# Attention and a two-layer MLP on one core: keys in four even tiles from the tenth pair on, in a newly drawn plan

## The chip, the core and the metric

One NeuronCore of a Trainium2 chip runs the whole program. Its engines work side by side, each through its own list of instructions in order: TensorE (PE) multiplies matrices, VectorE (DVE), ScalarE (ACT) and GpSimd (POOL) work on elements, and SyncE (SP) issues transfers, as ACT and POOL can too. Engines wait for each other by semaphores. The metric is the device time of one execution in microseconds (us). The kernel before took 692.31 us, the median of 3 runs (692.15 to 693.16).

## What is computed

```python
def _attn_ref(q, k, v, cap):                      # q, k, v: 4 x 12 heads x 448 x 64
    scale = 1.0 / np.sqrt(q.shape[-1])
    scores = scale * np.matmul(q, k.transpose(0, 1, 3, 2))
    scores = cap * np.tanh(scores / cap)          # cap = 30
    scores = scores - np.max(scores, axis=-1, keepdims=True)
    attn = np.exp(scores)
    attn = attn / (np.sum(attn, axis=-1, keepdims=True) + 1e-09)
    return np.matmul(attn, v)

def _moe_ref(x, w_in, w_out):                     # x: 1792 x 768, w_in: 768 x 2048, w_out: 2048 x 768
    h = x @ w_in
    g = np.maximum(0.01 * h, h)
    return g @ w_out
```

The heads of a batch, laid side by side, are the rows of x.

## The kernel before

**Pairs.** Two heads make a pair; there are 24, six for each of the four batches. Head 0 of a pair stands on partitions 0 to 63 of a tile, head 1 on 64 to 127. Keys and queries are loaded in 32-column pieces and turned on DVE (kT, qT, 128 x 448). The scores are computed with keys on the partitions, so that tanh (`L414`) and exp (`L416`) on ACT write the probabilities `pf` just as the product with the values needs them. 448 keys are three tiles of 128 and a rest of 64. For the three, one matmul for each head reads half of the partitions (`L406`, two side by side); the two rests share one tile: `kb` is a block matrix with both rests on its diagonal, and one full 128 x 128 matmul (`L403`) makes their scores. Values come in eight blocks (`vc`, four DMAs); for each of the four tiles two matmuls of 64 columns add to `po0` (`L434`). The sums of exp are added up on DVE or POOL in `t` (`L450` to `L454`) and multiplied with ones on PE (`L459`, `po1`). DVE turns the sums, takes the reciprocal, turns it back and scales (`L467` to `L479`).

**The MLP.** It runs in single-pass matmuls (`m`, `L543`) on numbers split into a rounded part and the rest: x into xh and xl, g into gh and gl, weights into two parts in `w` (`split`, the helpers `L234`, `L238` and `L241`: a cast on ACT or DVE, then a subtraction on DVE or POOL). Three products for each 128 rows. A unit is one block of 128 columns of the first layer (six blocks of rows, 18 matmuls) or one block of the second for a chunk of 5 or 6; 34 units a batch, 136 in all. In the first batch a weight is loaded raw (`wr`), its bits rearranged by ACT and DVE (`L528` to `L535`), and stored to `scratch`, from where later batches load it (`ws`). ACT or DVE makes 0.01 h (`L578`), DVE the maximum (`L583`); second-layer blocks are accumulated in `late` (`L592`), turned (`L600`) and stored by SP in four DMAs (`L605`).

**The order** is no scheduler's on the chip: class `Plan` lays it out while the program is built. Each step is added with a rank (a due time by pair or unit, shifted by the tables `role`, `pair` and `unit`), the engines that could do it, a cost for each, what it reads and writes, and a `mode` (the tiling of PE that its matmuls need). `issue` repeats: of the steps whose inputs are there, take the one that can start first (in steps of 0.1 us, then by rank), on the engine where it would end first, with the penalties in `phases` added for some engines; a step of PE in another mode than the last costs `SWITCH` more. What comes out is one fixed list for each engine. Rings of buffers (`raw` 3, `kT` 2, `w` 4, `pf` 4, `g` 11 and so on) say how far a step may run ahead of its reader.

Of the kernel before, what the change touches and what calls it, by code (L numbers as in the profile page):

```python
# [14 lines left out]
ALU = mybir.AluOpType  # L15
# [9 lines left out]
    pf=4,  # L25
# [29 lines left out]
    phases=[(-496.0, 3.97, 0.03), (5863.0, 0.58, 1.0), (1000000000.0, 7.89, 3.45)],  # L55
# [7 lines left out]
class Plan:  # L63
# [9 lines left out]
    SWITCH = 10  # L73
# [93 lines left out]
def softcap_attention_mlp(  # L167
# [87 lines left out]
    ring("vx", 2, [P, 4, 3, D])  # L255
# [83 lines left out]

    way = lambda i: "whole" if i < T["np"] else "beside"  # L340
# [37 lines left out]
    def plan_pair(i):  # L378
        plan.part("pair", " zero" if i == 0 else " first" if i < NP else "", i)
        r0 = 10.0 * i  # L380
        how = way(i)
# [10 lines left out]
        for j in range(2):  # L392
            plan.add(r0 + T["pk"] + 1, {"dve": 0.15, "act": 0.25, "pool": 0.5}, lambda e, j=j: copy(
                e, at("kb", i)[half[j], half[j]], at("kT", i)[half[j], mid_keys[j]], zeros[half[j]]), [("kT", i)], [("kb", i)])
        plan.add(r0 - T["al"] + 1, {"sp": 1.05 if how == "whole" else 2.1}, lambda e: load_v(i), [("fixed_vx", 0)], [("vx" if how == "whole" else "vc", i)], xfer=1.05)

        last = []
        for g in range(NG):
            ver = NG * i + g

            def scores(e, g=g, ver=ver):
                if g == MID:
                    nc.tensor.matmul(at("sc", ver)[:, 0, 0:S], at("kb", i), at("qT", i), start=True, stop=True)  # L403
                    return
                for j in range(2):
                    nc.tensor.matmul(at("sc", ver)[:, j, 0:S], at("kT", i)[half[j], tile_keys(j, g)], at("qT", i)[half[j]], start=True, stop=True)  # L406

            plan.add(r0 + T["pq"] + 2 * g, {"pe": BOTH}, scores, ([("kb", i)] if g == MID else [("kT", i)]) + [("qT", i)], [("sc", ver)], mode=int(g != MID))
            n = 1 if g == MID else 2
            sc = lambda ver=ver, n=n: at("sc", ver)[:, 0:n, 0:S]  # L410
            pf = lambda ver=ver, n=n: at("pf", ver)[:, 0:n]
            r = r0 + T["pt"] + 2 * g
            ct = 0.15 + 0.37 * n
            a = plan.add(r, {"act": ct}, lambda e, sc=sc, pf=pf: nc.scalar.activation(pf(), sc(), AF.Tanh, scale=inv_sb),  # L414
                         [("sc", ver), ("inv", 0)], [("pf", ver)])
            plan.add(r, {"act": ct + 0.03}, lambda e, pf=pf: nc.scalar.activation(pf(), pf(), AF.Exp, scale=cap_sb), (), [("pf", ver)], after=[a])  # L416


            r = r0 + T["pp"] + 2 * g
            if how == "whole":  # L420
                def values(e, g=g, ver=ver):
                    for j in range(2):
                        c = slice(0, P) if g < MID else half[j]
                        t = at("vx", i)[c, (g if j == 0 else g + 1) if g < MID else (3, 0)[j], j:j + 2]
                        nc.tensor.matmul(at(f"po{j}", i)[:, 0:S], t.rearrange("p o d -> p (o d)"), at("pf", ver)[c, j if g < MID else 0],
                                         start=(g == 0), stop=(g == MID))

                last = [plan.add(r, {"pe": 2 * BOTH if g < MID else BOTH + 0.1}, values, [("vx", i), ("pf", ver)], [("po0", i), ("po1", i)],
                                 after=last, mode=int(g == MID))]
            else:  # L430
                def values(e, g=g, ver=ver):
                    for j in range(2):
                        c = 3 + j if g == MID else g + 5 * j
                        nc.tensor.matmul(at("po0", i)[half[j], 0:S], at("vc", i)[:, c], at("pf", ver)[:, j if g < MID else 0],  # L434
                                         start=(g == 0), stop=(g == MID))
# [312 lines left out]
```

## Time and profile before

| | us |
|---|---|
| median of 3 runs | 692.31 |
| the profiled execution, its own time | 692.5 |
| its span (first to last instruction in the trace) | 690.7 |
| PE busy, share of the span | 668.9, 97% |
| DVE busy | 459.5, 67% |
| ACT busy | 416.2, 60% |
| POOL busy | 90.3, 13% |

Matmuls are pipelined, and the ends in the trace are modelled: how much PE really does is read from start to start. An fp32 matmul of the attention shows as two records, those of the MLP as one.

### The profile page before, as it was taken

Reading aid. Unit: us, or ns where it says so; the run is one execution under the profiler, and the core shown is the slowest. Engines: PE = TensorE matmul, PEld = TensorE weight load, DVE = VectorE, ACT = ScalarE, POOL = GpSimd, SP = SyncE. Lnnn points to the kernel's source line nnn. Section 1 sums busy time; section 2 is a strip of 40 time slices with the busy share of each in tenths; the row PEclk is TensorE's granted clock in tenths of the full one; section 3 lists DMA queues with packets and bytes.
Section 4 is the critical chain, followed back from the end, with each engine's and each line's share of the span. In section 5 each row is a group of like instructions: output and inputs, shape, how many; then the busy total and the mean of one; then the engine's idle time right before and its main releaser. Section 6 shows DMA issues by size and latency. Waiting matters only on the chain.

```text
span 690.7 us, 9078 instructions
## 1 busy us (share of the span) xinstructions
PE 668.9 (97%) x3136; PEld 496.3 (72%) x3136; DVE 459.5 (67%) x667; ACT 416.2 (60%) x612; POOL 90.3 (13%) x115
## 2 busy tenths in 40 slices
PE   8898999999999999999999999999999999999994
PEld 4234657766778557557888977788987499999983
DVE  4987999799989768775465547544456657345552
ACT  5997989798787777775452435544326625444330
POOL 8422221014200521220000000000000000000000
PEclk9999999999999999999999999999999999999998
DMA  9988879887885847533223254522333146333324
GB/s 137 195 139 210 224 224 269 274 222 220 227 277 196 191 105 137 121 88 106 92 92 109 80 128 121 150 87 87 103 102 94 37 119 176 95 121 107 100 54 68
DMA packets 173925, 98.20 MB, mean 142 GB/s; under 512 B 130864, under 2 KB 155440, under 8 KB 173872
## 3 DMA queue, kind: packets, MB, share of 16 engines
q1 hardware_dynamic: 169968, 93.65, 52.2%
q0 software_dynamic: 2048, 3.67, 2.8%
q8 instruction: 26, 0.43, 0.3%
q10 hardware_dynamic: 1856, 0.23, 0.3%
q14 instruction: 27, 0.22, 0.1%
HBM read 79.43 MB, written 18.09 MB: 141 GB/s over the span
## 4 chain that ended last, share of the span: by engine, by line
PE 82%; ACT 7%; DVE 5%; DMA 3%; issue 1%; ACTq 0%; DVEq 0%
PE m L543 64%; PE po L434 8%; PE sc L406 6%; PE sc L403 2%; ACT pf L414 2%; PE po L459 2%; ACT pf L416 1%; DVE wr L532 1%; DMA wr<-in_moe_w_in_dram 1%; DVE w L241 1%; DMA vc<-in_v_dram 1%; DVE ws L535 1%; ACT ws L530 1%; ACT wr L528 1%; ACT w L234 1%
## 5 line engine op out<-in xcount | busy, mean ns | idle before, releaser
L543 PE MATMUL m<-xh,w 128*128 128x448 f32 x768 | 231.8, 374 | 1.2 <-DVE late L583 1.1
L543 PE MATMUL m<-gh,w 128*128 128x448 f32 x768 | 229.4, 371 | 0.8 <-DVE w L241 0.6
L241 DVE TENSOR_TENSOR w<-ws,w 128x768 fp32r<-128x768 f32 (+1 forms) x135 | 127.4, 948 | 83.9 <-ACT w L234 76.8
L234 ACT CAST w<-ws 128x768 fp32r<-128x768 f32 (+1 forms) x130 | 102.6, 795 | 130.5 <-PE m L543 115.1
L543 PEld LDWEIGHTS m<-xh,w 128*128 128x128 f32 x768 | 145.0, 189 | 29.5 <-issue 7.1
L543 PEld LDWEIGHTS m<-gh,w 128*128 128x128 f32 x768 | 144.1, 188 | 29.4 <-issue 9.4
L543 PE MATMUL m<-gl,w 128*128 128x448 f32 x384 | 140.4, 366 | 1.2 <-DVE gl L241 1.2
L543 PE MATMUL m<-xl,w 128*128 128x448 f32 x384 | 140.9, 367 | 0.0
L414 ACT ACTIVATE pf<-sc,inv_sb 128x896 f32<-128x896 f32 (+1 forms) x87 | 76.6, 911 | 11.1 <-PE po L434 5.1
L416 ACT ACTIVATE pf<-pf,cap_sb 128x896 f32<-128x896 f32 (+1 forms) x87 | 80.2, 950 | 0.4
L543 PEld LDWEIGHTS m<-gl,w 128*128 128x128 f32 x384 | 72.2, 188 | 7.7 <-DVE gl L241 1.5
L543 PEld LDWEIGHTS m<-xl,w 128*128 128x128 f32 x384 | 72.6, 189 | 7.1 <-issue 1.5
L406 PE MATMUL sc<-qT,kT 64*128 64x448 f32 x288 | 68.0, 573 | 6.5 <-ACT pf L414 4.5
L434 PE MATMUL po<-pf,vc 128*64 128x448 f32 x348 | 74.2, 549 | 0.0
L578 ACT ACTIVATE late<-m 128x448 f32<-128x448 f32 x64 | 34.6, 542 | 42.2 <-PE m L543 38.4
L592 DVE TENSOR_TENSOR late<-m,late 128x448 f32<-128x448 f32 x48 | 29.5, 618 | 43.1 <-PE m L543 42.8
L583 DVE TENSOR_TENSOR late<-m,late 128x448 f32<-128x448 f32 x64 | 39.4, 617 | 26.9 <-ACT late L578 26.7
L406 PEld LDWEIGHTS sc<-qT,kT 64*128 64x128 f32 x288 | 23.3, 185 | 40.1 <-issue 13.4
L434 PEld LDWEIGHTS po<-pf,vc 128*64 128x64 f32 x348 | 22.3, 136 | 41.1 <-issue 35.0
L347 POOL DMA_DIRECT2D qraw<-in_q_dram x64 | 40.3, 636 | 74.6 <-DVE qT L370 48.1
L241 DVE TENSOR_TENSOR gl<-late,gh 128x448 fp32r<-128x448 f32 x61 | 38.5, 636 | 17.0 <-ACT gh L234 16.5
L234 ACT CAST gh<-late 128x448 fp32r<-128x448 f32 x55 | 31.0, 565 | 27.3 <-DVE late L583 26.8
(62 smaller groups left out, 504.6 us busy)
## 6 DMA issues: line engine op xcount, KB each, us to landing
ws<-scratch SPq DMA_DIRECT2D x66, 384.0 KB, 3.1
wr<-in_moe_w_in_dram SPq DMA_DIRECT2D x16, 768.0 KB, 6.5
ws<-scratch SPq DMA_DIRECT2D x36, 320.0 KB, 2.9
scratch<-ws SPq DMA_DIRECT2D x22, 384.0 KB, 5.6
wr<-in_moe_w_out_dram SPq DMA_DIRECT2D x12, 640.0 KB, 5.0
kraw<-in_k_dram SPq DMA_DIRECT2D x96, 56.0 KB, 3.4
vc<-in_v_dram SPq DMA_DIRECT2D x48, 96.0 KB, 3.9
wr<-in_moe_w_out_dram SPq DMA_DIRECT2D x6, 768.0 KB, 7.0
```

Of the source, the lines that this page charges most:

```text
L234: nc.scalar.copy(o, i)
L241: ENG[eng].tensor_tensor(out=o, in0=a, in1=f32(b), op=ALU.subtract)
L347: engine.dma_start(out=t[p0:p0 + 32], in_=src[b, 2 * hp + h, :, 32 * x:32 * x + 32].rearrange("(s i) d -> i s d", i=32),)
L403: nc.tensor.matmul(at("sc", ver)[:, 0, 0:S], at("kb", i), at("qT", i), start=True, stop=True)
L406: nc.tensor.matmul(at("sc", ver)[:, j, 0:S], at("kT", i)[half[j], tile_keys(j, g)], at("qT", i)[half[j]], start=True, stop=True)
L414: a = plan.add(r, {"act": ct}, lambda e, sc=sc, pf=pf: nc.scalar.activation(pf(), sc(), AF.Tanh, scale=inv_sb), [("sc", ver), ("inv", 0)], ...
L416: plan.add(r, {"act": ct + 0.03}, lambda e, pf=pf: nc.scalar.activation(pf(), pf(), AF.Exp, scale=cap_sb), (), [("pf", ver)], after=[a])
L434: nc.tensor.matmul(at("po0", i)[half[j], 0:S], at("vc", i)[:, c], at("pf", ver)[:, j if g < MID else 0], start=(g == 0), stop=(g == MID))
L543: nc.tensor.matmul(o, l, r, start=(first and m == 0), stop=(last and m == len(mm) - 1))
L578: nc.scalar.mul(at("g", f), ps(), 0.01)
L583: plan.add(rank, {"dve": 0.54}, lambda e: nc.vector.tensor_tensor(out=at("g", f), in0=ps(), in1=at("g", f), op=ALU.max), [("m", m)], [("g" ...
L592: op = plan.add(rank, {"dve": 0.54}, lambda e: nc.vector.tensor_tensor(out=acc(), in0=ps(), in1=acc(), op=ALU.add), [("m", m)], [(tag, b)] ...
```

## The change

From pair 9 on (`ev=9`) the 448 keys of a head are four tiles of 112. Scores are eight matmuls on halves in two steps of the plan (four matmuls each), without `kb`; tanh and exp always take two times 448 columns; t takes three wide additions; values (eight matmuls) and sums (two) are one step; v is one DMA. The branch `whole`, which was off (`np=0`), and its buffers `vx` are gone; the ring `pf` has six buffers of its own for four. In the plan a change of mode costs 0.2 us where it cost 0.1; the penalties are given by engine, in four phases, and their limits now fall inside the program; all tables of shifts have other numbers. The last two DMAs of the last output go out by ACT's queue.

```diff
-    pf=4,
+    pf=6,
...
-    np=0,
...
-    phases=[(-496.0, 3.97, 0.03), (5863.0, 0.58, 1.0), (1000000000.0, 7.89, 3.45)],
+    phases=[(40.0, {'pool': 0.43, 'dve': 0.3, 'act': 5.66}), (100.0, {'pool': 0.21, 'dve': 0.5, 'act': 0.05}), (200.0, {'dve': 0.51, 'act': 0.33, 'sp': 5.98}), (1000000000.0, {'dve': 0.5, 'sp': 14.02})],
+    ev=9,
...
-    SWITCH = 10
+    SWITCH = 20
...
+    KT = S // NG
+    even = lambda i: i >= T["ev"]
...
+        if even(i):
+            rows = v[b, 2 * hp:2 * hp + 2].rearrange("h s d -> (h s) d").rearrange("(c p) d -> p c d", p=KT)
+            nc.sync.dma_start(out=at("vc", i)[0:KT], in_=rows)
             return
...
+        K = KT if even(i) else P
+        wide = lambda g: 2 if even(i) or g < MID else 1
+        pf = lambda g: at("pf", NG * i + g)[0:K, 0:wide(g)]
...
+        def scores(g):
+            if wide(g) == 1:
+                nc.tensor.matmul(at("sc", NG * i + g)[:, 0, 0:S], at("kb", i), at("qT", i), start=True, stop=True)
+                return
+            for j in range(2):
+                keys = slice(KT * g, KT * g + KT) if even(i) else tile_keys(j, g)
+                nc.tensor.matmul(at("sc", NG * i + g)[0:K, j, 0:S], at("kT", i)[half[j], keys], at("qT", i)[half[j]], start=True, stop=True)
...
+        for gs in ((0, 1), (2, 3)) if even(i) else ((0,), (1,), (2,), (3,)):
+            keys = [("kT", i)] if wide(gs[0]) == 2 else [("kb", i)]
+            plan.add(r0 + T["pq"] + 2 * gs[0], {"pe": len(gs) * BOTH}, each(scores, gs), keys + [("qT", i)], vers("sc", gs), mode=int(wide(gs[0]) == 2))
...
+        if even(i):
+            def all_values(e):
+                each(values, range(NG))(e)
+                total(e)
+
+            plan.add(r0 + T["pp"] + 7, {"pe": (NG + 1) * BOTH}, all_values, vers("pf", range(NG)) + [("vc", i), ("t", i), ("fixed_vx", 0)], [("po0", i), ("po1", i)], mode=2)
...
                 for r in range(4):
-                    nc.sync.dma_start(
+                    queue = nc.scalar if m == B * NU - 1 and r >= 2 else nc.sync
+                    queue.dma_start(
```

On PE, in the middle of the program, the steps of a pair between two runs of m matmuls (sc are scores, with kT on halves of the array and with kb on the whole of it; po are values, and sums where ones stand). Before:

```order
L543 MATMUL m_159<-gh_138,w_134 128x448
L406 MATMUL sc_88<-qT_81,kT_79 128x448 x2
L406 MATMUL sc_89<-qT_81,kT_79 128x448 x2
L434 MATMUL po_0_90<-pf_94,vc_86 64x448 x2
L434 MATMUL po_0_90<-pf_95,vc_86 64x448 x2
L406 MATMUL sc_88<-qT_81,kT_79 128x448 x2
L403 MATMUL sc_89<-qT_81,kb_83 128x448
L459 MATMUL po_0_91<-t_96,ones 64x448 x2
L543 MATMUL m_159<-gh_139,w_134 128x448
```

And a pair at about the same place now:

```order
L533 MATMUL m_160<-gh_141,w_133 128x448
L406 MATMUL sc_86<-qT_81,kT_79 112x448 x2
L406 MATMUL sc_87<-qT_81,kT_79 112x448 x2
L411 MATMUL po_0_88<-pf_90,vc_84 64x448 x2
L411 MATMUL po_0_88<-pf_91,vc_84 64x448 x2
L411 MATMUL po_0_88<-pf_92,vc_84 64x448 x2
L411 MATMUL po_0_88<-pf_93,vc_84 64x448 x2
L415 MATMUL po_0_89<-t_96,ones 64x448 x2
L406 MATMUL sc_86<-qT_81,kT_79 112x448 x2
L406 MATMUL sc_87<-qT_81,kT_79 112x448 x2
L533 MATMUL m_159<-gh_137,w_134 128x448
```

Six changes of tiling for seven steps before, four for nine now; over the whole program 151 and 141.

On DVE, while the first units of the MLP run between the pairs 7 and 8 (late is g here, gh and gl its two parts, w the weight's). Before:

```order
L583 TENSOR_TENSOR late<-m_159,late 128x448
L535 SCALAR_TENSOR_TENSOR ws_131<-ws_131,wr_128 128x768
L241 TENSOR_TENSOR gl_151<-late,gh_140 128x448
L532 SCALAR_TENSOR_TENSOR wr_127<-wr_127 128x768
L241 TENSOR_TENSOR w_132<-ws_131,w_132 128x768
L583 TENSOR_TENSOR late<-m_160,late 128x448
L535 SCALAR_TENSOR_TENSOR ws_130<-ws_130,wr_127 128x768
```

Now, at the same work:

```order
L573 TENSOR_TENSOR late<-m_160,late 128x448
L469 TENSOR_TENSOR x_103<-po_0_88,sums_99 128x448
L238 CAST gh_142<-late 128x448
L238 CAST w_132<-ws_131 128x768
L241 TENSOR_TENSOR xl_121<-x_103,xh_110 128x448
L241 TENSOR_TENSOR w_132<-ws_131,w_132 128x768
L573 TENSOR_TENSOR late<-m_159,late 128x448
L367 STREAM_TRANSPOSE kT_78<-kraw_73 128x448
L238 CAST gh_141<-late 128x448
```

Casts that stood in ACT's list (gh, w) now stand in DVE's.

In the list of SP, the stores at the end of the program (out_dram is the output; late, kraw and qraw are the buffers that it is stored from). Before:

```order
L605 DMA out_dram<-late 32x14x32 x4
L605 DMA out_dram<-kraw_73 32x14x32 x4
L605 DMA out_dram<-late 32x14x32 x4
L605 DMA out_dram<-qraw_76 32x14x32 x4
L605 DMA out_dram<-kraw_74 32x14x32 x4
L605 DMA out_dram<-qraw_77 32x14x32 x4
```

Now:

```order
L596 DMA out_dram<-late 32x14x32 x4
L596 DMA out_dram<-kraw_73 32x14x32 x4
L596 DMA out_dram<-late 32x14x32 x4
L596 DMA out_dram<-qraw_76 32x14x32 x4
L596 DMA out_dram<-kraw_74 32x14x32 x4
L596 DMA out_dram<-qraw_77 32x14x32 x2
```

The other two of the last output stand behind ACT's last cast.

## Rows read from the trace of the kernel before

**Rows 1.** The page: span, and busy time by engine, its share, instructions.
```profile
span 690.7 us, 9078 instructions
PE 668.9 (97%) x3136; PEld 496.3 (72%) x3136; DVE 459.5 (67%) x667; ACT 416.2 (60%) x612; POOL 90.3 (13%) x115
```

**Rows 2.** Busy time by stretches: stretch, length, each engine (instructions), clock, DMA, GB/s.
```profile
0.00:143.00 143.00, 132.73 (x586) 76.44 (x588) 119.38 (x173) 123.04 (x174) 42.38 (x63) 0.99 0.92 208
143.00:225.00 82.00, 80.84 (x377) 57.07 (x374) 76.67 (x107) 66.36 (x100) 15.12 (x13) 1.00 0.76 231
...
300.00:551.00 251.00, 251.00 (x1199) 199.25 (x1199) 140.09 (x204) 123.66 (x184) 9.15 (x11) 1.00 0.35 99
551.00:691.00 140.00, 129.35 (x637) 118.72 (x633) 68.14 (x99) 48.23 (x75) 1.15 (x1) 0.97 0.40 104
```

**Rows 3.** PE's waits: who waited for whom, us in total, times, longest.
```profile
PE sc L406 <- ACT pf L414: 4.5, 3, 2.9
```

**Rows 4.** Timeline of ACT from 58 us: start, us, instruction, idle before.
```profile
58.18 0.94 ACT L530 ACTIVATE ws<-wr 128x768 f32<-128x768 f32 x1
62.58 0.90 ACT L528 ACTIVATE wr<-wr 128x768 int32<-128x768 uint8 x1 [3.46 <-DMA wr<-in_moe_w_in_dram]
```

**Rows 5.** Timeline of PE from 60 us.
```profile
64.42 1.02 PE L406 MATMUL sc<-qT,kT 64*128 64x448 f32 x4 [2.87 <-ACT pf L414]
65.37 0.47 PE L543 MATMUL m<-xh,w 128*128 128x448 f32 x1
...
69.83 0.54 PE L403 MATMUL sc<-qT,kb 128*128 128x448 f32 x1
```

**Rows 6.** Timeline of PE from 376 us.
```profile
376.58 0.36 PE L543 MATMUL m<-gl,w 128*128 128x448 f32 x1
376.78 0.37 PE L543 MATMUL m<-gh,w 128*128 128x448 f32 x1
377.08 1.77 PE L406 MATMUL sc<-qT,kT 64*128 64x448 f32 x8
378.78 0.47 PE L543 MATMUL m<-xh,w 128*128 128x448 f32 x1
379.09 0.37 PE L543 MATMUL m<-xl,w 128*128 128x448 f32 x1
```

**Rows 7.** Groups by line and shape: busy us, mean ns of one, idle before.
```profile
L416 ACT ACTIVATE pf<-pf,cap_sb 128x896 f32<-128x896 f32 x65 | 66.5, 1045 | 0.3
L414 ACT ACTIVATE pf<-sc,inv_sb 128x896 f32<-128x896 f32 x65 | 63.6, 1006 | 10.1 <-PE po L434 5.1 <-PE sc L406 4.6
...
L234 ACT CAST gh<-late 128x448 fp32r<-128x448 f32 x55 | 31.0, 565 | 27.3 <-DVE late L583 26.8
...
L416 ACT ACTIVATE pf<-pf,cap_sb 128x448 f32<-128x448 f32 x22 | 14.7, 670 | 0.1
L414 ACT ACTIVATE pf<-sc,inv_sb 128x448 f32<-128x448 f32 x22 | 13.9, 631 | 1.0 <-PE sc L403 0.9
...
L238 DVE CAST gh<-late 128x448 fp32r<-128x448 f32 x9 | 3.4, 382 | 0.1
```

**Rows 8.** Timelines of POOL and DVE near 175 us; w on DVE: min/median/max ns.
```profile
175.38 2.13 POOL L450 TENSOR_TENSOR t<-pf,pf 128x896 f32<-128x896 f32 x1 [8.54 <-issue]
...
175.43 2.76 DVE L241 TENSOR_TENSOR w<-ws,w 128x640 fp32r<-128x640 f32 x1
...
L241 DVE TENSOR_TENSOR w<-ws,w x135: 782/950/2760, 51.8 to 672.1; 128x768 fp32r<-128x768 f32 x88, 128x640 fp32r<-128x640 f32 x47
```

**Rows 9.** Timeline of PE, SP and DVE at the end; SPq is SP's issuing.
```profile
680.19 0.36 PE L543 MATMUL m<-gh,w 128*128 128x448 f32 x1
680.43 3.21 SPq L605 DMA_DIRECT2D out_dram<-kraw  x4
...
681.25 0.65 DVE L600 STREAM_TRANSPOSE qraw<-late 128x448 f32<-128x448 f32 x1
683.75 2.02 SPq L605 DMA_DIRECT2D out_dram<-qraw  x4
```

More of the change, by code (lines that the diff above doesn't have):

```diff
@@ L391, in plan_pair @@
                      [(nm + "raw", i)], [(nm + "T", i)], port=False)
[L392 to L397, printed above, removed]
@@ L398, in plan_pair @@
-        for g in range(NG):
[L399 to L411, printed above, removed]
-            r = r0 + T["pt"] + 2 * g
[L413 to L435, printed above, removed]
-                last = [plan.add(r, {"pe": BOTH}, values, [("vc", i), ("pf", ver)], [("po0", i)], after=last, mode=2)]
@@ new lines, in plan_pair @@
+        plan.add(r0 - T["al"] + 1, {"sp": 0.55 if even(i) else 2.1}, lambda e: load_v(i), [("fixed_vx", 0)], [("vc", i)], xfer=1.05)
+        if not even(i):
+            for j in range(2):
+                plan.add(r0 + T["pk"] + 1, {"dve": 0.15, "act": 0.25, "pool": 0.5}, lambda e, j=j: copy(
+                    e, at("kb", i)[half[j], half[j]], at("kT", i)[half[j], mid_keys[j]], zeros[half[j]]), [("kT", i)], [("kb", i)])
+        K = KT if even(i) else P
+        wide = lambda g: 2 if even(i) or g < MID else 1
@@ new lines, in values, with total, each, do @@
+        def values(g):
+            for j in range(2):
+                c = NG * j + g if even(i) else 3 + j if g == MID else g + 5 * j
+                nc.tensor.matmul(at("po0", i)[half[j], 0:S], at("vc", i)[0:K, c], pf(g)[:, j if wide(g) == 2 else 0], start=(g == 0), stop=(g == NG - 1))
+        def total(e):
+            for j in range(2):
+                nc.tensor.matmul(at("po1", i)[half[j], 0:S], ones[0:K], tt()[:, j], start=True, stop=True)
+        def each(fn, gs):
+            def do(e):
+                for g in gs:
+                    fn(g)
+            return do
@@ new lines, in plan_pair @@
+        WIDE = {"dve": 1.0, "pool": 2.25}
+        r = r0 + T["pt"] + 3
+        a = plan.add(r, WIDE, lambda e: ENG[e].tensor_tensor(out=tt(), in0=pf(0), in1=pf(1), op=ALU.add), vers("pf", [0, 1]), [("t", i)])
+        for g in range(2, NG):
+            if wide(g) == 2:
+                a = plan.add(r + 2 * g - 2, WIDE, lambda e, g=g: ENG[e].tensor_tensor(out=tt(), in0=tt(), in1=pf(g), op=ALU.add), vers("pf", [g]), [("t", i)], after=[a])
+                continue
+            for j in range(2):
+                plan.add(r + 4, {"dve": 0.65, "pool": 1.3}, lambda e, j=j, g=g: ENG[e].tensor_tensor(
+                    out=tt()[half[j], j], in0=tt()[half[j], j], in1=pf(g)[half[j], 0], op=ALU.add), vers("pf", [g]), [("t", i)], after=[a])
@@ new lines, in plan_pair @@
+        if even(i):
[3 more added lines that the diff above has]
+            plan.add(r0 + T["pp"] + 7, {"pe": (NG + 1) * BOTH}, all_values, vers("pf", range(NG)) + [("vc", i), ("t", i), ("fixed_vx", 0)], [("po0", i), ("po1", i)], mode=2)
+        else:
+            last = []
+            for g in range(NG):
+                last = [plan.add(r0 + T["pp"] + 2 * g, {"pe": BOTH}, each(values, [g]), vers("pf", [g]) + [("vc", i)], [("po0", i)], after=last, mode=2)]
+            plan.add(r0 + T["pp"] + 7, {"pe": BOTH}, total, [("t", i), ("fixed_vx", 0)], [("po1", i)], mode=2)
@@ L472, in plan_pair @@
             [("rt", i)], [("sums", 2 * i + 1)], port=False)
[L473 to L481 removed]
+        plan.add(rn, {"dve": 0.54}, lambda e: nc.vector.tensor_tensor(
+            out=at("x", 2 * i + 1), in0=at("po0", i)[:, 0:S], in1=at("sums", 2 * i + 1), op=ALU.mult),
+            [("po0", i), ("sums", 2 * i + 1)], [("x", 2 * i + 1)], port=False)
         split(rn + 0.5, lambda: at("xh", i), lambda: at("xl", i), lambda: at("x", 2 * i + 1), S, [("x", 2 * i + 1)], ("xh", i), ("xl", i))
@@ L618, in softcap_attention_mlp @@
         setup()
-        plan.issue([(limit, {"pool": a, "dve": b, "sp": T["psp"]}) for limit, a, b in T["phases"]])
+        plan.issue(T["phases"])
     fast.close()
```

58 lines of the change are left out of this document (15 added, 43 removed).

## The prediction

> **What bounds the kernel now.** I read the page first: PE is busy for 668.9 of 690.7 us, DVE and ACT for about two thirds [rows 1]. So the question is where PE is not at work, and the table of busy time by stretches answers it [rows 2]. In the first 143 us PE is busy for 132.73 us, while ACT has 123.04 and DVE 119.38 us of work; in the 251 us from 300 on PE is never idle; the last stretch holds 10.65 us without PE, the end of the program. The three stretches have different limits: the first is paced by ACT and DVE, the middle by PE alone, the end by the stores. The table of PE's waits then says for whom: score matmuls wait for the tanh of ACT, 4.5 us in three waits [rows 3]. The timeline of ACT around the longest of them shows why: at 59.1 us ACT reaches the first step on a weight that has not landed and stands 3.46 us [rows 4]. PE stands for 2.87 us until 64.42, and then 12 m matmuls take from 65.37 to 69.83, 4.46 us, where 12 at 0.204 us take 2.45 [rows 5]: after this standstill TensorE ran some matmuls at its lower level (1.2 GHz), which cost 2.0 us more.
>
> The sum is made against the profiled execution: 690.7 us of span and 1.8 us around it, 692.5 us; the median shown, 692.31 us, is 0.2 us lower, within the spread of the three runs.
>
> **Changes of tiling on PE.** The same matmuls run before and after: where a pair had one 128x128 score matmul and six on halves, it now has eight on halves, and the planner counts both as four steps of 0.752 us. What changes is how often PE goes from one tiling of its array to another. Counted in the order of the two programs, there are 151 such changes before and 141 after (m and the full score matmul are one tiling, the scores on halves a second, values and sums a third). A change has its price in the trace: two m matmuls follow each other in 0.20 us, but the last one before the scores takes 0.30 and the first one after them 0.31; the two score steps between take 1.70 us [rows 6], one alone takes 0.95 (64.42 to 65.37 [rows 5]), so that a step more costs 0.75 and entry and exit the other 0.20. Together 0.10 + 0.11 + 0.20 = 0.41 us for two changes, 0.2 us each. Ten fewer: **-2.0 us**. The place matters: of the changes up to the first 100 us of PE's work, 41 become 52, and from there on 110 become 89. If the early ones lie under the wait for ACT, the gain is 21 x 0.2 = 4.2 us; that end goes into the range.
>
> **The first 143 us.** Up to the sums of pair 8, which end at 143.6 us, both programs put the same work before PE (42 steps of m, nine pairs), but not the same on the others: ACT has 174 instructions before and 152 after, DVE 166 and 186. Casts of g, accumulations and kb copies went over. A cast on ACT is 0.565 us and on DVE 0.382 us [rows 7], a mean instruction of the stretch 0.71 us on ACT (123.04 over 174) and 0.69 on DVE (119.38 over 173) [rows 2]. So ACT loses between 12.4 and 15.6 us by these two prices, less for the kb copies, which are shorter: I take 10. DVE gains between 20 x 0.382 = 7.6 and 20 x 0.69 = 13.8 us; I take 10, nearer the cast, the commonest of them. That makes about 113 us for ACT and 129 for DVE in a stretch of 143: DVE takes ACT's place as the fuller of the two, 90% where ACT was at 86%. If DVE idles as long as now (143 - 119.4 = 23.6 us), the stretch gets 10 us longer. If it closes its idle time with the added work, nothing is lost. On the other side stands the wait of ACT: in SP's queue 23 groups of loads stood before the weight of unit 3 and 18 do now (two of k and three of v are behind it instead), while ACT comes to it only slightly earlier. That is five groups of about 2 us earlier, so most of the 3.46 us and of the 2.0 us of slow matmuls should go. Against it, ahead of the last exp of pair 5 ACT now has eight steps on weights instead of three, and fewer others: by the mean of 0.71 us at most 3.6, of which I count 2 us. Gain 5.4, loss 2, and of DVE's 10 us a third, 3: **-0.5 us**, between -7 (all waits of rows 3 and the slow matmuls, nothing lost) and +10.
>
> Beside this stands a rule of the Trainium skill (SBUF - State Buffer, section "SBUF: two separate sides"): the port pair that VectorE and GpSimd share is an exclusive lock, and whoever comes second is blocked for the whole instruction of the other. The trace agrees: a subtraction of DVE that began 0.05 us after a 2.13 us addition on POOL took 2.76 us [rows 8], where the shortest of its kind takes 0.78 and the median 0.95. It speaks against a change that gives 22 more weight subtractions to POOL; but up to pair 8 POOL's additions become fewer (t 6 to 5, xl 2 to 0), and the 22 lie where DVE has room, so by this rule the stretch would rather gain a few us on DVE than lose.
>
> **112 keys in a tile.** From pair 9 on a pair has four tanh and four exp of 2 x 448 columns, where it had three of each and one of 448. A pair costs ACT 1006 - 631 + 1045 - 670 = 750 ns more [rows 7], 11.3 us for 15 pairs, less the two kb copies of a pair that are gone. PE does not see it: its steps go by columns. From 143 us on ACT's share falls with every stretch, 48.23 of 140 us in the last [rows 2], and the change takes over a hundred instructions from it, so I cost this at nothing. Were that cover gone in pairs 9 to 14, it would be 6 x 0.75 = 4.5 us. The loads of v become one DMA for four on SP, which relieves the queue and ends nothing.
>
> The Trainium skill says the same as a warning (Trainium Kernel Development and Optimization, section "Best Practices"): always tile to 128 partitions. By it the 11.3 us stand; by the rows they lie on an engine that is waited for only early, where the tiles stay as they are.
>
> **The end.** The last matmul starts at 680.19, the last output is turned at 681.25 + 0.65 = 681.9, but its four stores start only at 683.75, because SP is at the four of the unit before from 680.43 to 683.64 [rows 9]. Now two of the last four stand in ACT's queue, which is free at that time. If SP's half waits as now, the last issue is 2 x 0.5 us earlier: -1.0. If the unit before is also stored in time (its matmuls now end 3.05 us before the end without pieces of another in between, and the stores before it start earlier), the issue ends at 681.9 + 1.05 instead of 685.77: -2.8. If the transfers themselves set the end: 0. I take **-1.5 us**.
>
> **The sum:** 692.5 - 2.0 - 0.5 - 1.5 = 688.5 us. The likeliest case alone reaches from 686.5 to 690.5.
>
> **Rivals.** First, the other side: DVE becomes the bound of the first 143 us. Mechanism: DVE keeps its order, and its added casts stand in front of transposes and sums that PE waits for. For it: 90% of the stretch booked, and DVE already at 76.67 of 82 us in the stretch after it [rows 2]. Against it: 23.6 us of idle time, part of which is only waiting for the ACT that is now earlier. With DVE's 10 us in full: 688.5 + 7 = 695.5 us, and with the ACT wait still there 701. It turns slower than before when DVE can hide less than 3 of the 10 us. Chance 0.20. Second: the early waits go altogether, and the changes of tiling count only late: 692.5 - 7 - 4.2 - 1.5 = 679.8 us at the best; with ACT's 2 us before pair 5 and 2 us of other waits left, 684. For it: the weight loads are earlier and ACT is lighter. Against it: transposes and the first loads have not moved, and somebody will be last. Chance 0.18. Third: nothing measurable. The ten changes saved are paid back under a wait, the stores end where the transfers end, and the first stretch gains nothing: 691 to 693 us. For it: PE stood for only 10 us in that stretch, and the page's other idle time is at the end. Chance 0.10. Fourth: the 112-row tiles come due in pairs 9 to 14: 688.5 + 4.5 = 693 us. ACT is at 66.36 of 82 us in the stretch after 143 [rows 2], so 16 us are free there even before any cast leaves it. Chance 0.02, counted as no change. That leaves 0.50 for the forecast.
>
> **How the numbers follow.** A measurement of this kernel tells about 0.2% (1.4 us) from no change: faster means under 690.9 us. The forecast and the second rival make 0.68 for faster, the third and fourth 0.12 for the same, the first 0.20 for slower. The range for 8 in 10 takes the forecast, the third and fourth, half of the second and half of the first: 684 to 695 us.
>
> **What would show it.** In the profile after: isolated score steps still at 0.95 us and values and sums in one run of ten matmuls; a table of PE's waits without the 2.9 us behind a tanh, and no m matmuls at the lower clock near 65 us; the sums of pair 8 ending between 141 and 145 us, with DVE near 129 us of work up to there; the last issue of a store over at most 4.6 us after the last matmul's start, where it was 685.77 - 680.19 = 5.6. I am wrong if PE now waits for DVE's transposes, casts or t in the first 230 us for more than 5 us, or if the stores end as late as before.

## The result: 696.91 us, 0.75% slower

The changed kernel takes 696.91 us (median of 4 runs, 696.65 to 698.53) beside 692.23 us for the kernel before (4 runs on the same chip): ratio 1.0075, 95% interval 1.0061 to 1.0090. The forecast was 688.5 us, with a range of 684 to 695. The profiled execution is the longest of the four, 698.53 us with a span of 696.7; what is compared below is its span with the 690.7 us of before, 6.0 us apart where the medians are 4.7 apart.

The page after, answering to [rows 1]: span, and busy time by engine.
```profile
span 696.7 us, 8964 instructions
PE 670.1 (96%) x3166; PEld 494.3 (71%) x3166; DVE 489.2 (70%) x733; ACT 367.4 (53%) x497; POOL 113.7 (16%) x129
```
ACT has 49 us less work and DVE 30 us more; PE's busy time is no shorter. The busy time by stretches, answering to [rows 2]:
```profile
0.00:143.00 143.00, 132.02 (x575) 72.91 (x576) 124.13 (x192) 114.00 (x151) 36.79 (x57) 0.99 0.94 216
143.00:225.00 82.00, 79.31 (x379) 56.18 (x378) 77.45 (x114) 66.76 (x90) 18.20 (x21) 1.00 0.76 220
...
300.00:551.00 251.00, 251.00 (x1213) 198.63 (x1212) 157.33 (x235) 96.61 (x136) 25.01 (x17) 1.00 0.34 96
```
Up to 143 us ACT has 9 us less (10 were counted) and DVE 5 more (10 were counted). The middle is still PE's alone. PE's waits, answering to [rows 3]:
```profile
PE sc L406 <- ACT pf L430: 3.4, 3, 1.6
PE sc L406 <- DVE qT L367: 1.8, 1, 1.8
PE m L295 <- DVE gh L293: 1.7, 1, 1.7
PE m L533 <- DVE late L582: 1.4, 1, 1.4
PE po L411 <- DVE x L469: 1.2, 2, 0.9
PE m L533 <- DVE late L573: 1.2, 2, 0.9
```
The long wait near 61 us is gone; instead there are more short ones, several of them for DVE. The slow matmuls at 65 us [rows 5] are gone from there too, but not from the program: TensorE is at the lower of its two clock levels from 35.2 to 38.6 us now, behind a wait for the tanh. Eight score matmuls take 2.97 us there, where eight take 1.77 in [rows 6]; the second line is the same stretch with PE's busy time, instructions, granted clock, DMA share and GB/s.
```profile
34.81 2.97 PE L406 MATMUL sc<-qT,kT 64*128 64x448 f32 x8 [1.60 <-ACT pf L430]
35.20:38.60 3.40, 3.40 (x12) 0.51 1.04 263
```

No group of rows shows where 6.0 us went. But all matmuls are in the traces, so the distances between their 3136 and 3166 starts can be added up, from the first score on. Each distance is split. The work is 0.2027 us for an m matmul, 0.188 for one on halves (values and sums too) and 0.375 for one of a full score tile. What an m matmul takes beyond that while under 0.23 us is called "pitch". Other excess is a "change" up to a distance of 0.7 us and a "wait" beyond; the excess of matmuls at the lower clock is counted with the waits. The columns e1 to e14 are runs of the next section.
```
us                    before   after      e1      e7      e9     e14
before the first        7.73    8.27    8.52    8.11    8.03    7.82
work                  629.20  629.23  629.23  629.61  629.61  629.61
pitch of m              1.18    4.54    5.31    1.74    0.85    1.79
changes                29.37   25.30   26.06   26.83   26.19   26.54
waits                  12.72   16.03   13.02   12.84   12.74   13.17
after the last starts  10.53   13.38   11.73   11.36   14.18   10.30
span                   690.7   696.7   693.9   690.5   691.6   689.2
```
Against before, the changes are 4.1 us less; the pitch is 3.4 more, the waits 3.3, the end 2.9 and the beginning 0.5. Of the waits' 3.3 us, 2.0 stand between 143 and 225 us, where m matmuls wait for DVE. They differ between executions of the new order on PE: in this stretch the waits are 3.7 us here, 1.25 in e1 and e14, 3.1 in e7 and 4.5 in e5, while each of the five traces with the old order has 1.7. Mostly they are long where PE comes early: e7 ends the sums of pair 8 1.6 us before e1 and waits 1.9 us longer up to 225 us.

**Pitch.** The stretch from 560 to 620 us holds m matmuls alone in both kernels, at a granted clock of 1.00. First before, then after (stretch, length, PE busy, instructions, clock, DMA, GB/s):
```profile
560.00:620.00 60.00, 60.00 (x298) 1.00 0.46 125
```
```profile
560.00:620.00 60.00, 60.00 (x292) 1.00 0.46 121
```
After, there are six fewer in the same 60 us. From start to start it is 202.67 ns on the mean of the 586 distances that the last run of before begins with, and 206.66 ns on all 934 of the last run after: 934 x 4.0 ns = 3.7 us, with the same instruction and the same clock.

**The end.** The rows answer to [rows 9] (SPq and ACTq are the issuing of SP and ACT):
```profile
681.33 0.65 DVE L590 STREAM_TRANSPOSE kraw<-late 128x448 f32<-128x448 f32 x1
683.37 0.37 PE L533 MATMUL m<-gh,w 128*128 128x448 f32 x1
684.43 0.65 DVE L590 STREAM_TRANSPOSE qraw<-late 128x448 f32<-128x448 f32 x1
685.11 1.47 ACTq L596 DMA_DIRECT2D out_dram<-qraw  x2
687.70 1.91 SPq L596 DMA_DIRECT2D out_dram<-kraw  x4
689.71 0.96 SPq L596 DMA_DIRECT2D out_dram<-qraw  x2
```
ACT issues its two DMAs as soon as the last output is turned. But SP, whose kraw has been turned since 681.98, issues nothing until 687.70. The waits of SP's queue from 670 us on say for whom:
```profile
SPq L596 <- DVE late L590: 7.4, 1, 7.4
SPq L596 <- DMA out_dram<-qraw: 4.4, 1, 4.4
```
SP waits 4.4 us for a DMA of qraw, the later unit, in the other queue. In the trace ACT's first DMA counts on semaphore 114 and lands at 687.63 us; SP stands at a wait for 114 and goes on at 687.65. The last issue ends 690.67 - 683.37 = 7.3 us after the last matmul's start; before it was 5.6.

### The profile page after: what moved, and what is told of

Its sections match the earlier page's. It is cut to its first block, busy times and chain, and to the rows that moved or that the text cites. A ratio compares the mean times of both kernels' runs of the same rounds, so it can differ in the third digit from the quotient of the medians.

```text
span 696.7 us, 8964 instructions
## 1 busy us (share of the span) xinstructions
PE 670.1 (96%) x3166; PEld 494.3 (71%) x3166; DVE 489.2 (70%) x733; ACT 367.4 (53%) x497; POOL 113.7 (16%) x129
## 4 chain that ended last, share of the span: by engine, by line
PE 79%; ACT 7%; DVE 6%; DMA 4%; issue 2%; SPq 0%; DVEq 0%; ACTq 0%
PE m L533 62%; PE po L411 8%; PE sc L406 7%; ACT pf L430 2%; PE po L415 2%; ACT pf L432 2%; DMA wr<-in_moe_w_out_dram 1%; DVE ws L525 1%; DMA wr<-in_moe_w_in_dram 1%; DMA vc<-in_v_dram 1%; DVE w L241 1%; ACT ws L520 1%; DVE wr L522 1%; DMA scratch<-ws 1%; DMA kraw<-in_k_dram 1%
## 5 line engine op out<-in xcount | busy, mean ns | idle before, releaser
L234 ACT CAST w<-ws 128x768 fp32r<-128x768 f32 (+1 forms) x80 | 62.9, 792 | 99.5 <-PE m L533 80.1
L430 ACT ACTIVATE pf<-sc,inv_sb 112x896 f32<-112x896 f32 (+2 forms) x90 | 84.4, 977 | 19.0 <-PE po L411 15.2
L432 ACT ACTIVATE pf<-pf,cap_sb 112x896 f32<-112x896 f32 (+1 forms) x90 | 88.3, 1015 | 0.1
L406 PE MATMUL sc<-qT,kT 64*112 64x448 f32 (+1 forms) x348 | 80.1, 572 | 6.4 <-ACT pf L430 3.4
L241 POOL TENSOR_TENSOR w<-ws,w 128x640 fp32r<-128x640 f32 (+1 forms) x23 | 38.3, 1664 | 239.5 <-PE m L533 111.2
L411 PE MATMUL po<-pf,vc 112*64 112x448 f32 (+1 forms) x360 | 74.1, 547 | 1.4 <-DVE x L469 1.2
L238 DVE CAST w<-ws 128x768 fp32r<-128x768 f32 (+1 forms) x56 | 30.1, 539 | 50.1 <-PE m L533 44.5
L406 PEld LDWEIGHTS sc<-qT,kT 64*112 64x112 f32 (+1 forms) x348 | 27.9, 178 | 44.7 <-issue 23.6
L582 DVE TENSOR_TENSOR late<-m,late 128x448 f32<-128x448 f32 x48 | 29.6, 620 | 35.9 <-PE m L533 35.9
L411 PEld LDWEIGHTS po<-pf,vc 112*64 112x64 f32 (+1 forms) x360 | 23.3, 136 | 42.9 <-issue 33.4
```

Source lines behind the costliest of these rows:

```text
L234: nc.scalar.copy(o, i)
L238: nc.vector.tensor_copy(o, i)
L241: ENG[eng].tensor_tensor(out=o, in0=a, in1=f32(b), op=ALU.subtract)
L406: nc.tensor.matmul(at("sc", NG * i + g)[0:K, j, 0:S], at("kT", i)[half[j], keys], at("qT", i)[half[j]], start=True, stop=True)
L411: nc.tensor.matmul(at("po0", i)[half[j], 0:S], at("vc", i)[0:K, c], pf(g)[:, j if wide(g) == 2 else 0], start=(g == 0), stop=(g == NG - 1))
L430: a = plan.add(r, {"act": ct}, lambda e, sc=sc, g=g: nc.scalar.activation(pf(g), sc(), AF.Tanh, scale=inv_sb[0:K]), vers("sc", [g]) + [("i ...
```

## Experiments

Every ratio is to the kernel before on the same chip. Five theories are tested: that (1) ACT's two DMAs at the end, (2) the pitch of the last run of m, (3) the even tiles, (4) the new tables or (5) ACT's table load behind the first tanh cost the time.

**e1, all stores on SP.**
```diff
-                    queue = nc.scalar if m == B * NU - 1 and r >= 2 else nc.sync
+                    queue = nc.sync
```


> The changed kernel with all four output DMAs of the last unit on SP again; nothing else differs. Theory 1 (tail): in the changed kernel SP stood from about 683.3 to 687.65 us before the fifth unit's DMAs, on a semaphore that ACT's first output DMA also counts, and the time after the last matmul's start grew from 10.53 to 13.38 us. Without ACT's two DMAs the last issue ends about 5.6 us after the last matmul's start again, and the time falls by 2.0 to 2.9 us, to about 694.4. Rival: the end is set by the last DMAs' own landing, which two queues share; then the time stays within 1 us of 696.9. Theory 2 (pitch): the last 936 weight matmuls ran 206.67 ns apart in the changed kernel and the last 633 of before 202.67 ns; where the program sets which of the two it is, this kernel shows 206.67 again, since TensorE's order is unchanged; where each execution draws it, it can be either, and 202.67 would be worth 3.7 us more.

696.09 us, ratio 1.0063 (1.0047 to 1.0079). The last issue ends 5.6 us after the last matmul's start again. The profile has 1.65 us less behind the last start, still 1.2 more than before, since SP's closing waits hold a gap of 1.07 us here that before does not have. By the ratios the time fell by 0.8 us, within their intervals and less than the 2.0 to 2.9 foretold: e1 alone does not decide between theory 1 and its rival, e2 does. The pitch of the last run is 206.66 ns again: the program sets it, not the execution.

**e2, the kernel before with ACT in the last store.**
```diff
-                    nc.sync.dma_start(
+                    queue = nc.scalar if m == B * NU - 1 and r >= 2 else nc.sync
+                    queue.dma_start(
```


> The kernel before with one edit: the last unit's third and fourth output DMA are issued by ACT instead of SP. Theory 1 (tail): SP's other stores then wait for ACT's DMA as in the changed kernel, and the time rises by 1 to 3 us, to about 694.5. Rival (what I forecast): two queues issue side by side, the last issue ends 1 to 2 us sooner, 690.7 to 692.2.

693.67 us, ratio 1.0029 (1.0018 to 1.0039), as theory 1 has it. SP's waits from 670 us on have the same row:
```profile
SPq L606 <- DMA out_dram<-qraw: 4.0, 1, 4.0
```
What I booked as a gain of 1.5 us costs 2.0 by itself.

**e3, no even tiles; e4, the old tables.**
```diff
-    ev=9,
+    ev=24,
```


> The changed kernel with no pair in even tiles (all 24 pairs keep the 128-row tiles and four value steps); its tables are those of the changed kernel. Theory 3: the even tiles save TensorE some 6 us (short matmul starts and changes: 659 us before, 656 us after, of which the slower pitch hides 3.4), so this kernel is 3 to 8 us slower than the changed one, 700 to 705. Rival: the even tiles are what costs (112 rows, ten matmuls that wait for all four groups); then it is 692 to 696.


```diff
-    pf=6,          (e4: also role, pair, unit and phases as before)
+    pf=4,
-    SWITCH = 20
+    SWITCH = 10
```


> The changed kernel (even tiles from the tenth pair on, ACT in the last store) with the tables of the kernel before: its role, pair and unit numbers, its two prices by phase, 10 for a change of form and four own buffers of pf. Theory 4: the new tables' beginning is what costs (the waits of 0.7 us and longer grew by 5.6 us, most of them in the first 60 us); then this kernel has the first 60 us of before and ends at 688 to 693. Rival: the tables cost nothing by themselves and old numbers fit the new steps worse; then 697 or more.

e3: 706.11 us, 1.0200 (1.0183 to 1.0218); e4: 705.41 us, 1.0196 (1.0180 to 1.0212). In e3, changes take 38.9 us instead of 25.3; in e4, waits take 22 us, spread from the first scores to 560 us. Theory 3 holds in direction: with these tables the even tiles are worth 1.25%. Theory 4 fell, its rival stands: the old numbers fit the new steps worse than the new ones. Both runs undo one half of a plan, and so measure the misfit with it, not the half alone.

**e5, ACT's table load first; e6, pair 0's kb copies on ACT** (both with all stores on SP, so they are compared with e1).
```diff
         nc.vector.memset(zeros, 0.0)
+        nc.scalar.copy(first_act, zeros)
```


> The changed kernel with all stores on SP, and one more instruction: ACT copies the column of zeros at the start, before anything of pair 0. Theory 5 (table load): in the changed kernel ACT's first activation is a tanh that waits for the scales of DVE until 9.31 us, and ACT's 1.28 us table load stands behind that wait, so the first tanh starts at 10.60 us; before, ACT's first activation was a copy of kb, the table load ran at 2.84 us and the first tanh started at 8.80 us. Then here the table load is done by 5 us, the first tanh starts near 9.4 us, and the kernel ends up to 1.2 us sooner than the one without the copy if ACT holds up TensorE in the beginning. Rival: the beginning is bound by DVE, the waits behind ACT come back as waits for DVE, and the time is that of the kernel without the copy within 0.5 us.


```diff
-                    e, at("kb", i)[half[j], half[j]], ...
+                    "act" if i == 0 else e, at("kb", i)[half[j], half[j]], ...
```


> The changed kernel with all stores on SP, and the two small copies of pair 0's kb on ACT, as before the change, instead of on DVE (the order of everything else is kept). Theory 5: the table load moves ahead of the copies, both qT turns start 0.39 us sooner, the first scores start near 8.1 instead of 8.52 us and the first tanh near 9.2 instead of 10.60 us; 1 to 1.6 us off the time if the beginning is bound by ACT. Rival (DVE bound): 0.4 us or nothing.

ACT's timeline at the start, after and in e6:
```profile
9.20 1.28 ACT L430 ACT_TABLE_LOAD   x1 [9.20 <-DVE bound L308]
10.49 1.91 ACT L430 ACTIVATE pf<-sc,inv_sb 128x896 f32<-128x896 f32 x2
```
```profile
2.86 1.28 ACT L234 ACT_TABLE_LOAD   x1 [2.86 <-issue]
7.39 0.50 ACT L234 COPY kb<-kT 64x64 f32<-64x64 f32 x2 [3.25 <-DVE kT L367]
9.01 1.91 ACT L430 ACTIVATE pf<-sc,inv_sb 128x896 f32<-128x896 f32 x2 [1.12 <-DVE small L309]
```
The first tanh is 1.5 us earlier in e6. Yet the sums of pair 8 end at 144.53 us (144.98 in e1), the waits from there to 225 us are 0.6 us longer than in e1, and the time is 695.69 us, 1.0070 (1.0045 to 1.0096): no gain on e1 that can be measured. The first row is PE's longest wait in e1, the second in e6:
```profile
PE sc L406 <- ACT pf L430: 3.7, 3, 1.6
```
```profile
PE po L411 <- DVE x L469: 2.6, 2, 1.7
```
What ACT gained, DVE takes: 0.9 us of waits for x became 2.6, while those for the tanh fell from 3.7 to 2.1. That is what the rival said. e5 (696.88 us, 1.0078, 1.0053 to 1.0102) loses the gain earlier, to the first loads: the table load runs at 0.75 us, amid ACT's own issues of qraw, and the first scores start at 9.56 instead of 8.52 us.

**e7, e9 and e10, one small matmul ahead of the last run** (e7 with all stores on SP, e9 with ACT's as in the change, e10 on the kernel before).
```diff
                 total(e)
+                if i == B * NP - 1:
+                    nc.tensor.matmul(tiles["sc"][0][0:64, 0, 0:64], ones, ones, start=True, stop=True)
```


> The changed kernel with all stores on SP and one small extra matmul (128x64 weights, 64 columns, its result unused) on TensorE behind pair 23's sums, just ahead of the last 936 weight matmuls. Theory 2 (pitch): which of the two pitches a run of weight matmuls keeps is settled where it begins; another beginning settles it anew, for 202.67 ns with a chance of about 3 in 4 by the runs of weight matmuls seen so far, and the last run then takes 3.7 us less; with 206.67 ns again the time is that of the kernel without it plus 0.1 to 0.3 us. Rival: the pitch follows from the kernel (where its weights and tiles lie), then it is 206.67 ns again.

> The changed kernel as it is, ACT's two output DMAs included, with the one small extra matmul (result unused) ahead of the last 936 weight matmuls. Theory 2 (pitch): the last run keeps 202.67 ns as in the kernel with all stores on SP, and the time falls by 3.6 us against the changed kernel, to 0.1 to 0.3% above before. Theory 1 (tail): it stays 1 to 2.5 us above the kernel that has the extra matmul and all stores on SP (ratio 1.0007), so near 1.003; the fifth unit's SP issues stand until ACT's first DMA has landed.

> The kernel before with the same small extra matmul behind pair 23's sums, ahead of its last 633 weight matmuls, which ran at 202.67 ns. Theory 2 (pitch): the extra matmul itself costs 0.1 to 0.3 us; if the run begins in the slower pitch now, 2.4 us more. So 691.2 or 693.6, by the pitch that the trace shows. Rival (the extra matmul helps by something else than the pitch, which would help here too): 1 us or more below before.

e7: 692.16 us, 1.0007 (0.9988 to 1.0027). e9: 693.95 us, 1.0030 (1.0018 to 1.0042). e10: 692.42 us, 1.0006 (0.9994 to 1.0019). PE's timeline at the beginning of the last run, after and then e7:
```profile
490.04 0.47 PE L533 MATMUL m<-xh,w 128*128 128x448 f32 x1
490.35 0.36 PE L533 MATMUL m<-xl,w 128*128 128x448 f32 x1
490.55 0.57 PE L533 MATMUL m<-xh,w 128*128 128x448 f32 x2
490.96 0.37 PE L533 MATMUL m<-xl,w 128*128 128x448 f32 x1
491.17 0.57 PE L533 MATMUL m<-xh,w 128*128 128x448 f32 x2
```
```profile
489.32 0.28 PE L451 MATMUL sc<-ones 128*64 128x64 f32 x2
489.53 0.47 PE L535 MATMUL m<-xh,w 128*128 128x448 f32 x1
489.84 0.36 PE L535 MATMUL m<-xl,w 128*128 128x448 f32 x1
490.04 0.57 PE L535 MATMUL m<-xh,w 128*128 128x448 f32 x2
490.45 0.36 PE L535 MATMUL m<-xl,w 128*128 128x448 f32 x1
490.65 0.36 PE L535 MATMUL m<-xh,w 128*128 128x448 f32 x1
```
From the first xl, three matmuls later is 0.61 us later in both (490.35 to 490.96, 489.84 to 490.45); the next three, from xh to xh, take 0.62 (490.55 to 491.17) and 0.61 (490.04 to 490.65). So it goes on, 206.66 and 202.67 ns on the mean of 934 distances. An instruction whose result nobody uses takes 3.9 us off (e7 against e1) and 3.1 (e9 against the change); the profiles of the same pairs have 3.6 and 3.7 us less pitch in the table. The rival falls. Where the run was fast anyway, it gives nothing (e10). And e9 against e7 is the price of ACT's two DMAs alone: 0.23%, 1.6 us, with intervals that overlap a little; the two profiles have 14.18 and 11.36 us behind the last start.

**e8, nine of them in the last run** (all stores on SP).
```diff
             def mm(e, cs=cs):
+                if cs[0] == 0 and m in range(84, 133, 6):
+                    nc.tensor.matmul(tiles["sc"][0][0:64, 0, 0:64], ones, ones, start=True, stop=True)
```


> The changed kernel with all stores on SP and nine small extra matmuls (128x64 weights, 64 columns, results unused) in the last 936 weight matmuls, one ahead of every sixth unit, so that the last stretch begins anew nine times. Theory 2 (pitch): each piece keeps one pitch, and the pieces differ: about 3 in 4 at 202.67 ns, which takes 2.5 us off; the nine interruptions cost 0.2 to 0.4 us each, 2 to 3.5 us together, so that the time stays within 1.5 us. Rival: all pieces run at 206.67 ns, as where the layout of the tiles sets it; then the time rises by the 2 to 3.5 us.

696.16 us, 1.0067 (1.0046 to 1.0088), that of e1. The first 72 matmuls run at 206.59 ns, and the nine pieces behind the small ones, 60 to 120 matmuls each, all at 202.6 to 202.7. So the pitch gains 3.5 us on e1, and the nine interruptions cost as much: the time is the same.

**e11 and e13, the store of the last unit but one in another queue, on the kernel before; e12 and e14, the same on the changed kernel with e6's and e7's edits.** (e11, e12: ACT; e13, e14: GpSimd.)
```diff
+                    queue = nc.scalar if m == B * NU - 2 else nc.sync      (e13, e14: nc.gpsimd)
```


> The kernel before with the whole store of the last unit but one (four output DMAs) issued by ACT, the last unit's by SP. My forecast's reason was that two queues issue side by side: SP's last issues then need not stand behind the 3.21 us of the unit before, and end 1.85 us sooner, 689.4. Theory 1 (tail): the DMAs of both queues count on the same eight semaphores, two of them in turns here, so that one queue waits for the other's DMA to land (about 2 us); then nothing is gained or 1 to 2 us lost.

> The changed kernel with three edits: the small extra matmul ahead of the last run, pair 0's kb copies on ACT, and the store of the last unit but one on ACT, all others on SP. With the extra matmul alone the ratio to before was 1.0007. Theories 1, 2 and 5: the pitch stays at 202.67 ns, the kb copies are worth 0.4 us or nothing, the store 1.85 us or a loss of 1 to 2: between 0.997 and 1.002 of before.

> The kernel before with the whole store of the last unit but one issued by GpSimd, the last unit's by SP. GpSimd's loads of qraw count on semaphores 103 to 110, SP's and ACT's DMAs on 100, 102 and 112 to 117, and one of its issues takes 0.63 us. Theory 1, in the form that the shared semaphores are the loss: nothing waits for the other queue's landing now, the last unit's issues begin when it is turned, 1.85 us sooner than behind the unit before, and the time falls by 1 to 1.9 us, to a ratio of 0.9975 to 0.9985. Rival (any second queue costs as much as it saves, since the landing or the closing waits set the end): within 0.5 us of before, or later, as with ACT (1.0018).

> The changed kernel with the small extra matmul ahead of the last run, pair 0's kb copies on ACT, and the store of the last unit but one on GpSimd, all others on SP. With that store on ACT the ratio was 0.9999. Shared semaphores the loss: 1 to 2 us below that, a ratio of 0.997 to 0.9985, and the last issue ends about 4 us after the last matmul's start. Rival: 0.9999 again.

e11: 693.44 us, 1.0018 (1.0007 to 1.0028), a loss again, and again SP waits for the other queue:
```profile
SPq L606 <- DMA out_dram<-kraw: 4.5, 1, 4.5
```
e12: 692.30 us, 0.9999 (0.9984 to 1.0014). e13: 692.06 us, 1.0005 (0.9993 to 1.0016). e14: 689.17 us, 0.9963 (0.9950 to 0.9976). The end of e14:
```profile
677.89 2.51 POOL L598 DMA_DIRECT2D out_dram<-kraw  x4 [10.33 <-DVE kraw L592]
678.93 0.37 PE L535 MATMUL m<-gh,w 128*128 128x448 f32 x1
679.99 0.65 DVE L592 STREAM_TRANSPOSE qraw<-late 128x448 f32<-128x448 f32 x1
680.66 2.76 SPq L598 DMA_DIRECT2D out_dram<-qraw  x4
```
The two queues now work side by side, and the last issue ends 683.42 - 678.93 = 4.5 us after the last matmul's start. On the changed kernel GpSimd instead of ACT is worth 0.36%, 2.5 us; 1.6 of them stand behind the last start in the two profiles. In e12 SP waits 4.2 us for the other queue's DMA, in e14 no such wait is left: the shared semaphores, not the second queue, were the loss. On the kernel before (e13) the last issue also ends after 4.5 us (5.6 before), and the span behind the last start is 0.7 us shorter, but of the 1 to 1.9 us foretold no gain can be measured. e14 beats both kernels, by 2.5 us the one before.

## Why the prediction was wrong

The recorded sum was -4.0 us, the profiled execution says +6.0. Step by step:

- **Changes of tiling, -2.0: right in direction, half the size.** In the traces there are 150 before and 140 after; they and the runs' beginnings take 4.1 us less. Up to 143 us, 11 more of them cost 1.0 us; beyond, 21 fewer saved 5.1, 0.24 us each. The place mattered as the range had it (4.2).
- **The first 143 us, -0.5: +1.1, and +2.6 for the same work.** The sums of pair 8 end at 144.82 us, in the 141 to 145 foretold, against 143.68. But the work up to there is not the same, as the sum took it to be: by then PE had all four score tiles of pair 9 behind it before, and has two now, 1.5 us of matmuls less. The 2.9 us wait went; the slow matmuls in this execution only moved, from 66 to 35 us. Not seen was that the kb copies, moved to DVE, push the first qT turn back (first scores 8.27 instead of 7.73 us) and leave ACT's table load behind the wait of the first tanh. e6 mends both without a gain that can be measured, since waits for DVE take over: the mechanism of the first rival, at about a quarter of its 10 us. The 1.1 us by itself is no more than executions differ by: the sums of pair 8 end between 143.45 and 145.04 us in the five traces with the old order, and between 143.22 and 145.05 in nine with the new one.
- **From there to 225 us, at nothing: +2.0 us of waits for DVE** in this execution, -0.4 to +3.5 in the others of the new order.
- **112 keys in a tile, 0: right.** No wait of PE above 0.7 us after 225 us.
- **The end, -1.5 (-2.8 to 0): the step that failed.** The forecast named it a sign of being wrong if the stores end as late as before; the last issue ends 7.3 us after the last start, where it was 5.6. That ACT's queue is free was read from the trace; that its DMAs count on the semaphores that SP's next DMAs need was not asked. It costs 1.6 us (e9 against e7) to 2.0 (e2) instead of gaining; with it comes 0.85 us of a gap in SP's closing waits, which stays unexplained. The order of the changed program shows the sharing: HW4 and HW6 stand on both queues.
```
SP   L596 DMA out_dram<-kraw_74 32x14x32 [waits DMAHW4_49,DVE_49]
SP   L596 DMA out_dram<-kraw_74 32x14x32 [waits DMAHW6_49]
ACT  L596 DMA out_dram<-qraw_77 32x14x32 [waits DMAHW4_49,DMASW2_49,DVE_49]
ACT  L596 DMA out_dram<-qraw_77 32x14x32 [waits DMAHW6_49,DMASW3_49]
```
- **The term that was missing: +3.4 us of pitch** (3.1 and 3.9 by e9 and e7). I took 0.204 us for every m matmul from [rows 5, 6]. The trace of before could have told: its 56 runs of m already have both, 0.2027 and 0.2066; only its longest, 633 matmuls, is fast by its beginning.

With the changes beyond 143 us at -5.1, the steps make -5.1 + 2.6 + 2.0 + 2.9 + 3.5 = 5.9 of the 6.0 us (3.5 is the pitch from there on). The time came out on the first rival's side, and not by its mechanism: without the slower pitch and ACT's store (e7) the new plan takes as long as the old one.

## What to carry to other kernels

Where PE is never idle, count its matmuls in equal stretches of both traces before looking for waits: a pitch that differs by 2% is seen by no table of busy time or waits, and a small matmul at the head of a long run can set it. Before a DMA moves to a free queue, look at which semaphores both queues count on; a queue with its own (here GpSimd's) kept the gain. And a plan's numbers are tested with the steps they were drawn for, or not at all.

## What the runs showed of the hardware that was not expected

- Runs of m matmuls (128x128 weights, 448 columns) go at 202.67 or 206.67 ns from start to start at a granted clock of 1.00, and keep it until something interrupts them. Of 315 beginnings in six traces (before, after, e1 to e4) 81 led to the slower pitch: 22 of 146 behind scores, 59 of 169 behind values, sums or full score tiles. Behind a small matmul of 64 columns all 14 led to the faster (e7 to e10, e12, e14). The same program begins a run mostly alike in every execution: the last run was slow in after, e1, e5 and e6. What decides it stays open.
- TensorE is once at the lower clock level early in the program: from 66.1 to 69.5 us before (and at 65 to 66 us in the other four traces with the old order), from 35.2 to 38.6 us after, behind waits of PE of 2.87 and 1.60 us. Of the nine traces with the new order four have such a stretch, at 27 to 35 us, and five have none, with waits of PE that are hardly different. What decides it stays open.
- ACT's table load, 1.28 us, stands directly ahead of its first activation and behind that one's wait (9.20 us after, 2.84 before).
- SP's and ACT's DMAs count on the same eight semaphores (100, 102, 112 to 117), GpSimd's on eight others (103 to 110); SP's next DMA on one of them waited until ACT's had landed, 2.5 us after its issue.
